# Inverse transform of two batches on 193 columns for a token and its mirror, in a kernel of attention and a gated long convolution

## Chip, cores and metric

The kernel runs on one core of a Trainium2 chip. The metric is the device time of one execution in microseconds (us), lower is better. The core has TensorE (PE: matmuls, with PEld for the weight loads that run beside them), VectorE (DVE), ScalarE (ACT), GpSimd (POOL) and SyncE (SP, here the issuer of most DMAs). Each engine takes its own instructions strictly in program order and waits on semaphores for the others.

## What is computed

Four batches, eight heads, 768 tokens, head size 64. Heads 0, 2 and 6 attend causally to everything, the others to a window of 64 tokens and 4 sink tokens. The attention output `x` of shape (4, 768, 512) goes through a gated convolution over the tokens:

```python
a = softmax(mask(q @ k.T / sqrt(64)))
x = (a @ v).transpose(0, 2, 1, 3).reshape(B, S, 512)
x1, x2, x3 = split(x @ w_proj, 3)                  # 512 channels each
X2 = rfft(x2, axis=1); H = rfft(filter_fft, axis=0)
y = x1 * irfft(X2 * H, n=S, axis=1) * x3
out = y @ w_out
```

## The kernel before

The tokens are split into two halves of 384 (`HS`), the transform is done as matmuls with tables of cosines and sines. Work is cut into small named operations; a long list, `FAST`, names every one of them in the order in which it is issued, so each engine's queue is that list without the other engines' entries. A suffix picks the engine where there is a choice (`/v` VectorE, `/s` ScalarE, `/p` GpSimd) and `@0` to `@3` picks one of four PSUM slots of two banks. A slot is free again when its last reader is done.

For each pair of heads `n` (0 to 15, four to a batch):
- `lq`, `lk`, `lv` load q, k, v (SP); `cq`, `ck` or `cqk`, and `cv{n}`, convert them to bf16. Up to n = 7 PE turns q and k (`T{n}.a`, emptied by `E`); from n = 8 a DMA does (`T{n}`, L962, on SP).
- `sc` are the score matmuls (L990), `sb` adds masks by matmul for the first pairs, `ex` is the exponential on ScalarE, `mk`/`mr` are masks on VectorE, `vx`, `vs`, `ks` prepare window and sink entries.
- `at` is probabilities times values, `rec` and `nm` divide by the sums (L1067, VectorE) and give `attn`.
- `fd`, `fe` fold the two halves of the tokens (difference and sum); from n = 5 `fA`, `fS`, `fb`, `fr` go further. `W` (L1103 to L1111) transforms attn over the tokens, `We` empties it.
- `tn` transposes attn into `xT`: on PE up to n = 10, by a DMA on SP (L1132) from n = 11.

For each batch `b`:
- `X{b}.t.u` multiplies the transformed attention with the x2 columns of w_proj (L1154), `Xe` empties it, `sw` swaps two halves of one piece by DMA; `pa`, `pb`, `pc` multiply with the filter's spectrum `HAB` and leave `P`.
- for each block `cb` of 128 channels: `x1`, `x3` are the two other projections (L1189; `xs` empties x1, `g` multiplies with x3). `c{b}.{cb}.r` is the inverse transform (L1227), for r = 0 and 1: three matmuls with 384 columns of the table `Gi` each. Their sum and difference are the two halves of the tokens: `ce` copies the r = 0 part to SBUF, and two operations `cv{b}.{cb}.half` (L1238) add and subtract the r = 1 part straight from PSUM. `y` multiplies in the remaining factor.
- `o{b}.{i}` are the output matmuls (L1262), `oe` empties them, `st` stores them. The last token block of batch 3 is done in two halves of the columns (L1257).

In the opening, `lfilt` loads the filter and `lw{part}.{hh}` the six pieces of w_proj; these DMAs are issued by GpSimd and stand in its queue (L776, L784). Piece `lw1.*` is what `X` needs, `lw0.*` and `lw2.*` are for `x1` and `x3`. `fold1` and `fold0` (L797, L793) fold the filter on VectorE, `F` transforms it, `H` scales it into `HAB`. Eight matmuls with no use, `rest` (L586), follow the last output matmul. `gd0` to `gd4` check the softmax sums: three VectorE operations, one matmul (`gd3`, L669) and a VectorE operation that writes a word `other` (`gd4`, L674). Every engine reads that word at the end (L1314) and branches on it.

Of the kernel before, what the change touches and what calls it, by code (L numbers as in the profile page):

```python
# [68 lines left out]
cv1/s nm0/v ex2.0 lw1.1 Ge0/v Gt1@3 sc1.2@1 ex2.1 ks2/s vs1/v Gh0 sb1.2 vx1/s sc2.4@0 ex1.2 T3.0@2 T3.1 lq4 Ge1/v lk4
fd0/v E3.0/v lw1.0 ex2.4 lq6 sc2.3@3 at1.1@1 fe0/v sc2.2@0 at1.0 E3.1/v rec1 sb2.2 nm1/v ex2.3 W0.1@3 cv2/s cv3/p  # L70
vx3/s ex2.2 fe1/v tn0@2 W0.0 te0/s sc3.1@1 sb3.1 vx2/v fd1/v at2.0@0 ck5/p vs2/s sc3.0@2 at2.1 We0/v lv4 cq5/s ks3/s
T5.1@3 cq4/p sb3.0 T5.0 ex3.1 sc3.2@1 sb3.2 rec2 nm2/v fe2/p E5.0/v ck4/p E5.1/v ex3.0 Gh1 W1.0@0 lv5 ex3.2 T4.0@2
E4.0/s W1.1 tn2@1 lq7 vs3/v tn1@3 We1/s T4.1 te2/v sc5.0@1 sc5.1@0 lk6 te1/v at3.1@3 fold1 at3.0 E4.1/s fold0 rec3
ex5.0 F2.1@2 ex5.1 sc4.4@1 nm3/v F2.0 ex4.4 sc4.5@0 ex4.5 fd2/v fd3/p sc4.2@3 ex4.2 F0.1@1 W2.1@0 W2.0 H2.0/v fe3/p
H0.2/s We2/s H2.2/v F1.1@3 F0.0 W3.1@0 H1.2/s lw0.0 H0.1/s H2.1/v ks5/p W3.0 cq6/v mk4.2 We3/v F1.0 H0.0/s H1.1/s
sc5.2@2 sc4.3@1 ex4.3 cv4/v X0.2.1@0 lw0.1 X0.2.0 H1.0/v sc4.1@1 sc4.0@3 lw2.0 mk5.0 ex5.2 X0.1.0@2 Xe0.2/s cv5/v
X0.1.1 ex4.0 X0.0.1@0 ex4.1 mk4.1 ck6/v vx5/v tn3@3 lk7 mk4.0 vs5/v X0.0.0 Xe0.1/s te3/s mk5.2 T6.0@1 Xe0.0/s Hd1
cq7/p lw2.1 T7.0@2 T6.1 mk5.1 ck7/v T7.1 at5.1@3 H2.5 pb0.1/v E7.0/v Hd0 at5.0 E6.1/s sw0.0 rec5 at4.1@0 E6.0/s at4.0
# [15 lines left out]
ks11/v pa1.1/p sc10.2@2 vx10/s sc11.2@0 X1.0.0 g1.0 sw1.0 vs10/v vs11/v ex10.2 x11.2.0@1 pb1.1/v fe9/v lq14 Xe1.0/s
mr10 fb8/v mk10.0 fS9/v mk10.2 x11.2.1 o0.4.0@2 mk11.1 ex11.2 tn9@3 xs1.2/s at10.0@0 at10.1 mk11.0 lq13 mk11.2 fA9/v
x11.1.0@1 x11.1.1 o0.5.0 o0.4.1 o0.5.1 fb9/p vx11/s rec10 cqk12/s nm10/v at11.0@0 at11.1 fr9 te9/s fr8 fd10/p
x31.1.0@3 T12 oe0.5/s W9.1@2 W9.0 xs1.1/s pb1.2/v x31.1.1 rec11 nm11/v tn10@1 pc1.1/v We9/s W8.1@0 tn11 W8.0 te10/s
g1.1 pa1.0/v sc12.1@2 pa1.2/v sc12.4@3 x31.2.1@1 x31.2.0 We8/s sc12.0@0 fe10/v pc1.2/v fe11/p ex12.1 x12.0.0@2 g1.2
fS10/p fA10/p lk13 ex12.4 x12.0.1 ex12.0 x32.0.0@3 pb1.0/v lv12 fb10/p pc1.0/v xs2.0/s sc12.5@1 sc12.2@0 fd11/v
sc12.3@2 x32.0.1 ex12.5 c1.0.0@1 c1.0.1 ex12.2 fr10 fA11/v lq15 fS11/v W10.1@0 W10.0 ex12.3 fr11 c1.1.0@2 c1.1.1  # L100
fb11/p g2.0 ce1.0/s c1.2.0@3 We10/s ce1.1/s W11.0@0 cv1.0.1 cv13/p cv1.0.0 mk12.1 cv1.1.0 cv1.1.1 c1.3.1@1 cqk13/s
W11.1 c1.3.0 y1.1/v y1.0/v ce1.3/v lk14 We11/s c1.2.1 ce1.2/s cv1.3.0 X2.1.0@2 lk15 T13 cv1.3.1 cqk14/s cv1.2.1
cv12/s X2.0.0@0 X2.1.1 mk12.0 X2.0.1 x31.3.0@1 T14 mk12.2 Xe2.1/s x31.3.1 Xe2.0/s cv1.2.0 y1.3/v sc13.1@3 vs13/s
# [5 lines left out]
fA13/v x12.2.0 cv14/v sw2.0 vs14/s cv15/v x12.1.0@3 o1.2.0@0 tn13 xs2.2/s mk15.0 vx15/s st1.1 mk14.0 o1.3.0 fb13/v
vs15/v fb12/v x12.1.1 oe1.5/s W12.1@1 mr14 mk15.1 fr13 mk14.2 W12.0 o1.3.1 o1.2.1 vx14/s at14.0@2 xs2.1/s mk15.2  # L110
W13.1@3 W13.0 st1.5 We12/s at14.1 oe1.3/s at15.0@1 pc2.1/v pb2.2/v We13/s at15.1 rec14 rec15 pc2.2/p x32.1.0@0
x32.1.1 nm14/v c2.1.0@3 nm15/v c2.1.1 tn14 st1.3 ce2.1/s g2.1 cv2.1.1 cv2.1.0 c2.0.0@2 ce2.0/s c2.2.1@1 fd14/p y2.1/v
c2.3.1@0 fe15/p c2.3.0 c2.2.0 ce2.3/s fd15/v x32.2.1@3 cv2.3.1 cv2.3.0 fe14/p c2.0.1 x32.2.0 cv2.0.1 tn15 fS15/p
fS14/p fA14/p x32.3.1@0 cv2.0.0 x13.1.1@2 fA15/p ce2.2/s x13.1.0 g2.2 x32.3.0 xs3.1/s fr14 fb15/v y2.0/v fb14/v
W14.0@3 W14.1 x13.0.1@2 We14/s cv2.2.0 fr15 x13.0.0 W15.0@3 W15.1 cv2.2.1 x33.0.1@1 We15/v x33.0.0 y2.2/p X3.2.1@3
X3.2.0 xs3.0/s Xe3.2/s X3.1.1@2 y2.3/v g3.0 X3.1.0 X3.0.1@1 sw3.1 g2.3 Xe3.1/s sw3.0 X3.0.0 x13.2.1@0 pa3.1/v Xe3.0/s
o2.1.0@3 x13.3.0@2 o2.0.0 pa3.2/p x33.2.0@1 x13.2.0 pb3.1/p x13.3.1 pb3.2/v gd0 pc3.2/v o2.1.1 xs3.2/s pa3.0/v
pb3.0/v x33.2.1 x33.1.0@0 pc3.1/v o2.0.1 xs3.3/s g3.2 c3.0.0@2 pc3.0/p x33.1.1 c3.1.0@1 oe2.1/s ce3.0/s o2.4.0@3 g3.1
gd1 c3.0.1 c3.2.1@0 c3.1.1 c3.2.0 o2.5.0 cv3.0.1 cv3.0.0 c3.3.0@2 ce3.1/s gd2 cv3.1.1 cv3.1.0 y3.0/p o2.5.1 o2.4.1
ce3.2/s y3.1/p c3.3.1 cv3.2.0 st2.1 oe2.5/s o2.3.0@1 o2.2.0 cv3.2.1 o2.3.1 o2.2.1 ce3.3/s cv3.3.1 x33.3.1@0 oe2.3/s  # L120
cv3.3.0 x33.3.0 y3.2/v st2.5 st2.3 gd3@3 o3.0.0@2 o3.4.0@1 y3.3/v g3.3 gh o3.0.1 gd4 oe3.0/s o3.4.1 o3.1.0@0 o3.1.1
o3.2.0@3 o3.2.1 o3.3.0@2 oe3.1/s o3.3.1 oe3.4/v st3.0/v oe3.2/s oe3.3/s o3.5.1@1 st3.4/v st3.1/v oe3.6/s o3.5.0@0
oe3.5/s st3.6/s st3.2/v st3.3/v st3.5/v rest@3 late
"""
# [1274 lines left out]
```

## Time and profile before

| | |
|---|---|
| times of three runs | 185.31, 184.15, 185.63 us; median 185.31 |
| span of the profiled execution, first to last instruction | 182.1 us |
| the profiled execution's own time outside the span | not given by the page; the median is 3.2 us above the span |
| busy: PE, DVE, ACT, POOL | 172.8, 149.8, 145.3, 77.5 us |
| TensorE clock granted | 1.000 |

The views used are: the share of each engine; the chain of work that ended last (start, length, what); groups of instructions (line, engine, operation, output<-inputs, shape, count, then busy us, mean ns of one, then idle time ahead and who ended it); the timeline (start, length, engine, line, operation, then in brackets the wait ahead of it); stretches of the span with the busy time of each engine; DMA issues with their time to landing; and single lines with first and last start.

### The profile page before, as it was taken

Reading aid. Unit: us, or ns where it says so; the run is one execution under the profiler, and the core shown is the slowest. Engines: PE = TensorE matmul, PEld = TensorE weight load, DVE = VectorE, ACT = ScalarE, POOL = GpSimd, SP = SyncE. Lnnn points to the kernel's source line nnn. Section 1 sums busy time; section 2 is a strip of 40 time slices with the busy share of each in tenths; the row PEclk is TensorE's granted clock in tenths of the full one; section 3 lists DMA queues with packets and bytes.
Section 4 is the critical chain, followed back from the end, with each engine's and each line's share of the span. In section 5 each row is a group of like instructions: output and inputs, shape, how many; then the busy total and the mean of one; then the engine's idle time right before and its main releaser. Section 6 shows DMA issues by size and latency. Waiting matters only on the chain.

```text
span 182.1 us, 4374 instructions
## 1 busy us (share of the span) xinstructions
PE 172.8 (95%) x1684; PEld 103.6 (57%) x1700; DVE 149.8 (82%) x298; ACT 145.3 (80%) x196; POOL 77.5 (43%) x94
## 2 busy tenths in 40 slices
...
GB/s 159 356 203 287 294 257 200 204 290 230 232 224 166 184 228 198 116 214 142 265 217 200 150 231 166 123 208 243 228 153 112 184 0 0 58 2 119 127 277 184
DMA packets 78396, 33.83 MB, mean 186 GB/s; under 512 B 67618, under 2 KB 74786, under 8 KB 78370
## 3 DMA queue, kind: packets, MB, share of 16 engines
...
q10 hardware_dynamic: 146, 0.13, 0.2%
...
## 4 chain that ended last, share of the span: by engine, by line
PE 82%; DVE 8%; ACT 4%; DMA 3%; issue 1%
PE f_x_ps L1189 23%; PE f_X_ps L1154 12%; PE f_out_ps L1262 10%; PE f_c_ps L1227 9%; PE f_sc L990 8%; PE f_att L1050 7%; DMA f_qkT<-f_qk_bf 3%; PE f_qkT_ps L952 2%; PE f_sc L1001 2%; PE warm L454 2%; PE f_xt_ps L1123 2%; ACT f_pT L1007 1%; DVE f_HAB L691 1%; PE f_W_ps L1103 1%; PE f_W_ps L1105 1%
## 5 line engine op out<-in xcount | busy, mean ns | idle before, releaser
L1007 ACT ACTIVATE f_pT<-f_sc 128x1024 bf16<-128x1024 f32 (+3 forms) x68 | 58.5, 914 | 3.6 <-PE f_sc L990 2.0
L1189 PE MATMUL f_x_ps<-f_xT,f_wproj 128*128 128x384 bf16 x256 | 46.9, 326 | 0.0
L1189 PEld LDWEIGHTS <-f_wproj 128*128 128x128 bf16 x256 | 23.9, 98 | 17.4 <-issue 1.6
L990 PE MATMUL f_sc<-f_qkT 64*128 64x128 bf16 (+3 forms) x328 | 20.9, 242 | 2.4 <-DMA f_qkT<-f_qk_bf 1.4
L1154 PE MATMUL f_X_ps<-f_wproj,f_xh 128*128 128x512 bf16 x90 | 22.1, 379 | 0.6 <-issue 0.2
L544 POOL TENSOR_TENSOR f_fo<-f_attn 128x384 bf16<-128x384 bf16 x15 | 14.6, 990 | 18.4 <-DVE f_attn L1067 17.3
L1262 PE MATMUL f_out_ps<-f_wout,f_gy 128*128 128x512 bf16 x86 | 22.0, 379 | 0.3
L990 PEld LDWEIGHTS <-f_qkT 64*128 64x128 bf16 x328 | 11.4, 94 | 13.0 <-issue 7.9
L1238 DVE TENSOR_TENSOR turns<-angle,f_c_ps 128x384 bf16<-128x384 f32 x32 | 16.3, 550 | 2.6 <-ACT angle L541 1.3
L1227 PE MATMUL f_c_ps<-f_Gi,f_P 128*128 128x384 bf16 x96 | 18.2, 326 | 0.1
L1050 PEld LDWEIGHTS <-f_pT 128*128 128x128 bf16 x472 | 16.2, 97 | 2.4 <-issue 0.4
L1050 PE MATMUL f_att<-f_v_aug,f_pT 128*128 128x65 bf16 x392 | 17.0, 193 | 0.0
L541 ACT COPY f_o<-f_out_ps 128x1024 f32<-128x1024 f32 (+2 forms) x15 | 12.1, 818 | 6.2 <-PE f_out_ps L1262 5.1
L541 ACT CAST f_X<-f_X_ps 128x1024 bf16<-128x1024 f32 x12 | 12.1, 1016 | 4.9 <-PE f_X_ps L1154 4.9
L1067 DVE TENSOR_TENSOR f_attn<-f_att,f_recs 128x768 bf16<-128x768 f32 x16 | 15.1, 951 | 0.6
L544 POOL TENSOR_TENSOR f_P<-f_X,f_HAB 128x1024 bf16<-128x1024 bf16 x4 | 8.9, 2215 | 14.5 <-ACT f_X L541 14.5
L544 POOL TENSOR_TENSOR f_gy<-turns,f_gy 128x768 bf16<-128x768 bf16 x5 | 8.5, 1710 | 14.6 <-DVE turns L1238 14.6
L1154 PEld LDWEIGHTS <-f_xh 128*128 128x128 bf16 x96 | 8.9, 97 | 10.2 <-issue 0.5
L1262 PEld LDWEIGHTS <-f_gy 128*128 128x128 bf16 x92 | 8.5, 98 | 8.8 <-POOL f_uv L544 0.4
L541 ACT COPY angle<-f_c_ps 128x384 f32<-128x384 f32 x15 | 7.2, 478 | 7.7 <-PE f_c_ps L1227 5.4
L1227 PEld LDWEIGHTS <-f_P 128*128 128x128 bf16 x96 | 9.1, 98 | 6.0 <-issue 0.2
L537 POOL CAST f_qk_bf<-qk_ahead 128x768 bf16<-128x768 f32 (+1 forms) x9 | 8.0, 900 | 8.7 <-DMA qk_ahead<-in_k_dram 3.4
...
## 6 DMA issues: line engine op xcount, KB each, us to landing
...
out_dram<-f_o SPq DMA_DIRECT2D x17, 256.0 KB, 2.4
...
f_wproj<-in_moe_w_proj_dram POOLq DMA_DIRECT2D x6, 256.0 KB, 8.2
out_dram<-f_o SPq DMA_DIRECT2D x3, 512.0 KB, 4.4
```

Of the source, the lines that this page charges most:

```text
L537: nc.gpsimd.tensor_copy(out=out, in_=in_)
L541: nc.scalar.copy(out=out, in_=in_)
L544: (nc.gpsimd if now["engine"] == "p" else nc.vector).tensor_tensor(out, a, b, op)
L990: nc.tensor.matmul(sc[:, bank, col:col + 128 * cnt], lhsT=keys, rhs=qkT(n)[rows, 0, 128 * i:128 * (i + cnt)], start=(col == 0 or not biase ...
L1007: nc.scalar.activation(out=pT(n)[:, c, :, 0:w], in_=held[f"sc.{n}.{c}"][:, :, 0:w], func=AF.Exp, scale=SCALE)
L1050: nc.tensor.matmul(att[:, hh, 65 * i:65 * i + 65], lhsT=pT(n)[:, c, bank, col:col + 128], rhs=values, start=(z == 0), stop=(z == len(here) ...
L1067: nc.vector.tensor_mul(attn(n).rearrange("p i hh d -> p hh i d"), rows[:, :, :, 0:64], recs()[:, n][:, :, :, None].to_broadcast([128, 2, N ...
L1154: nc.tensor.matmul(ps[:, u, :], lhsT=xh(b)[:, cc, chain, 128 * part:128 * part + 128], rhs=wproj()[:, cc, DM:2 * DM], start=(cc == 0), sto ...
L1189: nc.tensor.matmul(ps[:, s, 0:HS], lhsT=wproj()[:, cc, part * DM + cb * 128:part * DM + (cb + 1) * 128], rhs=xT(b)[:, cc, s * HS:s * HS + HS],
L1227: nc.tensor.matmul(ps[:, r, 0:HS], lhsT=P(b)[:, t, u, ch], rhs=Gi()[:, tile_no], start=(m == 0), stop=(m == 2))
L1238: fn(conv[:, half * HS:half * HS + HS], held[f"evs.{b}.{cb}"], held[f"c_ps.{b}.{cb}"][:, 1, 0:HS])
L1262: nc.tensor.matmul(ps[:, i % 2, :], lhsT=gy(b)[:, cb, i * 128:(i + 1) * 128], rhs=wout()[:, cb, :], start=(cb == 0), stop=(cb == NC - 1))
```

## The change

For batches 2 and 3 the inverse transform is done on 193 columns. Its tables have symmetries: the value at token n and at its mirror, 768 - n, are the same up to sign, once cosine and sine terms are kept apart. So the first two of the three tables are used on columns 0 to 192 alone and give two partial results side by side in one bank, of 193 columns each. The third table holds cosines and sines in one tile (rows 0 to 63 and 64 to 127); a new table `Gb` (128 x 2 x 2 x 194, bf16) has its rows laid apart with zeros elsewhere, so that one matmul of 386 columns adds to both. `Gb` is made by a memset (`Gz`), two copies (`Gb0`, `Gb1`) and a correction of one row (`Gn`).

`ce` now copies 386 columns, the two `cv` write sum and difference of 386 columns each in fp32 to SBUF, and two new VectorE operations per block, `cw{b}.{cb}.half`, add and subtract the 193-column parts from each other, the second one reading backwards, and write `conv`. That is 16 operations more. They use the buffers of the first two loads of q and k.

The filter's real part is no longer stored twice in `HAB` for t = 0 and 1; `pa` reads it through a broadcast.

The core of the diff:

```diff
+    Gb = C("Gb", [128, 2, 2, 194], BF16)
...
+    wave = lambda part, rows, tiles: Gi()[rows, tiles].rearrange("p t m f -> p t (m f)")[:, :, 0:193]
+    @op("Gz")
+        (nc.gpsimd if now["engine"] == "p" else nc.vector).memset(Gb(), 0.0)
+    for half in range(2):
+        @op(f"Gb{half}")
+            rows = slice(64 * half, 64 * half + 64)
+            ev(Gb()[rows, :, half, 0:193], wave(half, rows, slice(2, 6, 3)))
+    @op("Gn")
+        nc.vector.tensor_copy(out=Gb()[64:65, 1, 0, 0:193], in_=wave(0, slice(64, 65), slice(5, 6))[:, 0])
+        nc.vector.memset(Gb()[64:65, 1, 1], 0.0)
...
-        scaled(f"H{t}.0", lambda t=t: HAB()[:, t, 0:2, :],
-               lambda t=t: FP(t)[:, 0, None, :].to_broadcast([128, 2, DM]), 2.0 / S)
+        scaled(f"H{t}.0", lambda t=t: HAB()[:, t, 0, :], lambda t=t: FP(t)[:, 0], 2.0 / S)
...
-                two(P(b)[:, t], held[f"X.{b}.{t}"], HAB()[:, t, 0:2], ALU.mult)
+                real = HAB()[:, t, 0:2] if t == 2 else HAB()[:, t, 0, None].to_broadcast([128, 2, DM])
+                two(P(b)[:, t], held[f"X.{b}.{t}"], real, ALU.mult)
...
+                    if b in MIRROR:                                   # MIRROR = (2, 3)
+                        both = ps[:, r, 0:386].rearrange("p (h n) -> p h n", h=2)
+                        nc.tensor.matmul(both, lhsT=P(b)[:, t2, u2, ch], rhs=Gb()[:, shared_tile // 3, :, 0:193],
+                                         start=True, stop=False, skip_group_check=True)
+                        nc.tensor.matmul(both[:, 0], lhsT=P(b)[:, t0, u0, ch], rhs=waves(a), start=False, stop=True, ...)
+                        nc.tensor.matmul(both[:, 1], lhsT=P(b)[:, t1, u1, ch], rhs=waves(z), start=False, stop=True, ...)
+                        return
...
+                        fn(parts[:, half, 0:386], even[:, 0:386], held[f"c_ps.{b}.{cb}"][:, 1, 0:386])       # cv
...
+                        if half == 0:                                                                       # cw
+                            two(conv[:, :, 0:192], parts[:, :, 0:192], parts[:, :, 193:385], ALU.add)
+                        else:
+                            two(conv[:, :, 192:384], parts[:, ::-1, 192:0:-1], parts[:, ::-1, 385:193:-1], ALU.subtract)
```

With this the whole list `FAST` is a new one: all operations stand in another order, and 130 of those that can run on several engines have another engine. The places that the prediction speaks of, old and new (three dots stand for other operations):

```diff
-... ck3/p ... cq3/p ... at0.0@3 at0.1 ... lfilt ... lw1.1 ... lw1.0 ... at3.1@3 fold1 at3.0 ... fold0 rec3 ... F2.1@2 ... nm3/v ... fe3/p ... X0.2.1@0
+... at0.0@3 at0.1 ... nm0/v ... ck3/p fd0/p ... cv2/p ... ks2/p ... Gz/p ... lfilt ... lw1.0 ... fold1 ... fold0 rec3 F2.1@3 ... nm3/v ... fd2/p ... fe3/p ... lw1.1 ... X0.2.1@0
-... cqk12/s nm10/v at11.0@0 ... T12 ... nm11/v ... tn11 ... sc12.1@2 sc12.4@3 ... sc12.0@0 ... x12.0.0@2
+... cqk12/p ... T12 ... nm11/v ... sc12.1@2 ... sc12.4@3 ... sc12.0@1 ... tn11 ... x12.0.0@2
+... fr13 We12/s c2.1.0@0 g2.1 c2.1.1 ce2.1/s cv2.1.1 cv2.1.0 cw2.1.1/v cw2.1.0/v c2.3.0@2 ... y2.1/v ... fr14 W14.0@3 cw2.3.1/v ... fr15 W14.1 cw2.0.1/v We14/s fb15/v W15.0@0 cw2.0.0/v W15.1 y2.0/p ...
+... pc3.0/v c3.1.1 ce3.1/s ... g3.1 cv3.1.0 cv3.1.1 cw3.1.1/v ... cw3.0.1/v ce3.3/s ce3.2/s y3.1/p y3.0/p cv3.3.0 ... cw3.2.1/v y3.2/v o3.4.0@3 y3.3/v g3.3 o3.0.0@2 o3.4.1 gh gd0 gd1 ...
-... gd2 ... gd3@3 o3.0.0@2 ... gh o3.0.1 gd4 ... o3.5.1@1 ... oe3.6/s o3.5.0@0 oe3.5/s st3.6/s st3.2/v st3.3/v st3.5/v rest@3 late
+... o3.3.1 st3.1/v oe3.3/s oe3.2/v o3.5.1@1 st3.2/v rest@2 st3.3/v gd2 gd3@2 oe3.6/v st3.6/s late gd4
```

More of the change, by code (lines that the diff above doesn't have):

```diff
@@ L69 @@
[L69 to L78, printed above, removed]
@@ L94 @@
[L94 to L103, printed above, removed]
@@ L109 @@
[L109 to L123, printed above, removed]
+ones1 kz2/v lq2 wrap0 sin2 ones0 blank3@2 alt size cos2 mtab3 ck0/s cq2/p T0.1@3 cq0/v cos1 gs0/v lk2 btab sin1 gs2/p
@@ new lines @@
+vx1/v lk5 lv3 fe0/v te0/v sb2.2 T3.1@0 lk4 E3.1/s T3.0 E3.0/v W0.1@3 Gh1 ex2.2 ck5/s W0.0 lfilt vs2/v lw1.0 at1.1@2
+vx2/p We0/v at1.0 rec1 sc3.1@0 sc3.0@1 sb3.0 ks3/p ex3.0 sb3.1 at2.1@3 at2.0 nm1/v cv3/p sc3.2@1 cq5/p ex3.1 sb3.2
+T5.0@2 T5.1 vx3/s ex3.2 fe1/v E5.1/s fd1/p W1.0@0 rec2 nm2/v E5.0/v ck4/p lq4 lk7 W1.1 We1/s tn2@1 te2/v cq4/p T4.1@3
+tn1@2 te1/v T4.0 E4.1/s lq6 sc5.0@0 lv5 fold1 sc5.1@1 vs3/p at3.0@2 E4.0/s ex5.0 at3.1 ex5.1 fold0 rec3 F2.1@3 ks5/p
+sc4.4@0 F2.0 sc4.5@1 nm3/v lq7 fe2/v fd2/p H2.1/v H2.2/v fe3/p sc4.2@2 ex4.4 F0.1@0 lw1.1 ex4.5 W2.0@1 H2.0/s F0.0
@@ new lines @@
+mk11.1 pa1.0/v x11.1.1@1 mk10.1 tn9@0 ex11.2 o0.5.1 vx10/p te9/s pa1.2/v fb9/v mk10.2 o0.4.1 x11.1.0 sw1.0 W9.0@0
+mk11.2 at10.1@3 oe0.5/s mr10 mk11.0 vs11/v xs1.1/s lk13 at10.0 rec10 x11.2.0@2 x11.2.1 xs1.2/s nm10/v W9.1 at11.1@1
+pb1.2/p at11.0 x31.1.0@3 x31.1.1 We9/s lv14 rec11 fd10/p nm11/v g1.1 cv14/s tn10@0 fe10/p W8.1@1 W8.0 pa1.1/v sc12.1@2
+lq15 te10/s fe11/v sc12.4@3 fd11/p We8/s fS10/v x31.2.0@0 fA10/v lk15 fb10/p sc12.0@1 x31.2.1 tn11 ex12.1 fS11/p
+ex12.0 pc1.2/v x12.0.0@2 lk14 lq14 x12.0.1 lv13 ex12.4 g1.2 xs2.0/s vx14/s x32.0.0@1 fr10 sc12.5@3 pb1.0/v pc1.1/v
```

106 lines of the change are left out of this document (78 added, 28 removed).

## Prediction

> **What bounds the kernel now.** I read the share of each engine first, then the chain that ended last, then stretches of the span, because a share over the whole span hides which engine ends a stage.
>
> ```profile
> PE 172.8 (95%) x1684; PEld 103.6 (57%) x1700; DVE 149.8 (82%) x298; ACT 145.3 (80%) x196; POOL 77.5 (43%) x94
> PE 82%; DVE 8%; ACT 4%; DMA 3%; issue 1%
> 139.80:151.50 11.70, 11.69 (x78) 7.27 (x76) 9.96 (x20) 4.31 (x7) 6.65 (x8) 1.00 0.42 80
> 151.50:164.10 12.60, 12.49 (x67) 6.55 (x68) 8.81 (x11) 5.65 (x7) 7.12 (x3) 1.00 0.09 21
> 164.10:172.30 8.20, 8.20 (x47) 4.30 (x46) 6.50 (x13) 3.64 (x6) 3.27 (x3) 1.00 0.35 130
> ```
>
> TensorE (PE) carries 82% of the chain. The three stretches run from the first inverse transform of batch 2 to the first output matmul of batch 3; after the length come busy us of PE, weight loads, VectorE (DVE), ScalarE (ACT), GpSimd (POOL), then the clock. PE is never free there, at full clock, and DVE is busy 25.3 of 32.5 us. So a matmul taken away pays here only as far as DVE's 7.2 free us carry what DVE is given.
>
> The opening is different. Where the chain crosses 30 to 40 us it runs through DVE, with two weight DMAs close behind:
>
> ```profile
> 30.88 1.02 DVE f_xT L535 x2
> 31.90 0.86 DVE f_fold L797
> 32.76 0.87 DVE f_fold L793
> 33.63 0.15 DVE f_recs L1056
> 33.81 0.96 DVE f_attn L1067
> ...
> 40.51 0.81 PE f_X_ps L1154 x3
> ```
>
> PE starts the spectrum of batch 0 (X0.2.1) at 40.51 only when this DVE row is through.
>
> The profiled execution has a span of 182.1 us; the median of the timed runs is 185.31. I take the 3.2 us between them as unchanged and sum against the span. Under 1% (1.85 us) a measurement of this kernel can't be told from no change.
>
> **Term 1, the matmuls: -2.6 us.** Each of the 16 inverse operations of batches 2 and 3 changes from three matmuls of 384 columns to one of 386 and two of 193.
>
> ```profile
> 96.48 1.30 PE f_x_ps L1189 x8
> 30.50 0.35 PE f_xt_ps L1123 x6
> 119.68 1.39 PE f_att L1050 x42
> ```
>
> The spacing is 162 ns for 384 columns (1.30/8), 58 ns for 128 (0.35/6) and 33 ns for 65, each of the last with its own weight load, so weights don't set a floor at 193. A straight line gives 163 ns for 386 and 82 ns for 193: 327 instead of 487 ns, 160 saved, 16 times 2.56 us. If 193 columns cost what 256 would by that line (109 ns), 1.7 us is left.
>
> **Term 2, VectorE in the last two batches: +1.8 us.** The sums and differences cv now write 386 fp32 columns, two more than before, which I cost at nothing. New are 16 operations cw on 2x192 fp32 elements, both inputs in SBUF, half of them reading backwards. The trace has none; the nearest rows:
>
> ```profile
> L1238 DVE TENSOR_TENSOR turns<-angle,f_c_ps 128x384 bf16<-128x384 f32 x32 | 16.3, 550 | 2.6 <-ACT angle L541 1.3 <-PE f_c_ps L1227 0.5 <-POOL f_gy L544 0.3
> L544 DVE TENSOR_TENSOR f_fo<-f_attn 128x384 bf16<-128x384 bf16 x17 | 6.8, 407 | 0.1
> L679 DVE SCALAR_TENSOR_TENSOR angle<-turns,angle 128x384 f32<-128x384 int32 x1 | 0.6, 557 | 0.7 <-ACT turns L462 0.7
> ```
>
> 384 elements take 407 ns in bf16 and 557 ns with two 32-bit inputs in SBUF. The cv average 510 ns a piece in busy time (16.3/32), overlap taken off; I take 0.50, nearest the 32-bit row, and keep 0.40 and 0.56 as ends. That is 8.0 us (6.4 to 9.0). The sequence also hands DVE pa3.2, pb3.1 and pc3.0, and takes y2.0, y2.3, fd15, fb14, We15 and the three guard steps gd0 to gd2 out of this stretch:
>
> ```profile
> L544 DVE TENSOR_TENSOR f_m<-f_X,f_HAB 128x1024 bf16<-128x1024 bf16 x7 | 4.7, 674 | 0.0
> L544 DVE TENSOR_TENSOR turns<-turns,f_x1s 128x768 bf16<-128x768 bf16 x4 | 2.3, 567 | 0.0
> L535 DVE CAST f_xh<-f_W_ps 128x768 bf16<-128x768 f32 x4 | 3.8, 956 | 1.6 <-PE f_W_ps L1107 1.5
> ```
>
> In: 3 x 0.67 = 2.0. Out: two y at 0.57, the fold fd15 at 0.40 (6.8/17), the smaller sum fb14 at 0.3, We15 at 0.96 and three guards on 192 elements, by the 407 ns row no more than 0.3 each: 3.7. DVE's demand becomes 25.3 + 8.0 + 2.0 - 3.7 = 31.6 us, while PE's stretch would shrink to 32.5 - 2.6 = 29.9. DVE becomes the bound: at least 1.7 of the 2.6 us comes back as PE waiting, and I write 1.8. With the cheap cw it is 0.1; DVE's own waits come on top (first rival). Behind a late cw stand conv, y, then the output matmuls; the weights of W14 and W15 wait behind it too, since fr14, fr15 and fb15 stand among the cw in DVE's queue.
>
> Small pieces cost nothing where I see cover: Gb0 and Gb1 are two ACT copies of half the rows, Gn two DVE operations, and the broadcast in pa replaces stored copies at equal width. H0.0 and H1.0 write half as much. If the cover fails, they are under 1 us together.
>
> **Term 3, the opening: +1.5 us.** The filter load lfilt moves behind fd0, cv2, ks2 and the new memset Gz in POOL's queue, and the weight load lw1.1 behind fe3, which waits for nm3.
>
> ```profile
> 17.33 1.59 POOL L537 CAST f_qk_bf<-qk_ahead 128x768 bf16<-128x768 f32 x2 [3.20 <-DMA qk_ahead<-in_k_dram]
> 18.86 1.04 POOL L776 DMA_DIRECT2D f_filt<-in_moe_filter_fft_dram  x1
> ...
> 34.91 1.78 POOL L544 TENSOR_TENSOR f_fo<-f_attn 128x384 bf16<-128x384 bf16 x2 [4.60 <-DVE f_attn L1067]
> 36.64 0.62 POOL L784 DMA_DIRECT2D f_wproj<-in_moe_w_proj_dram  x1
> f_filt<-in_moe_filter_fft_dram POOLq DMA_DIRECT2D x1, 768.0 KB, 12.7
> f_wproj<-in_moe_w_proj_dram POOLq DMA_DIRECT2D x1, 256.0 KB, 7.3
> f_wout<-in_moe_w_out_dram POOLq DMA_DIRECT2D x1, 512.0 KB, 5.5
> ```
>
> The filter landed at 18.86 + 12.7 = 31.6, and fold1 began at 31.8: no slack. POOL is held by a key load until 17.33 as before. One cast then takes 0.8; fd0 is a fold like those at 34.91 (0.9 each), and cv2, ks2 and Gz, a cast, a small copy and a memset, take together between one and three times that, so lfilt is issued between 20 and 22; I take 21. By 12.7 us it lands near 34; less stands behind it in its queue than the two weight loads of before, so I take 33, 1.2 us late. nm3 follows fold1 by 2.9 us (rows above), fe3 takes 0.9, so lw1.1 is issued near 37 and lands between 42.3 (5.5 us, the landing on a calm queue) and 44.1 (7.3). X0 needs both halves. Some 0.9 us of matmuls now stand ahead of X0.2.1 that stood behind it, so X0 would be due at 41.4; it is 0.9 to 2.7 late, and I take 1.5. The lower end is -1: with less on DVE and ACT ahead of the fold, the opening may gain if both loads come early.
>
> The Trainium skill ("DMA: Bandwidth & Descriptors", section "Anatomy of one DMA — SWDGE (gpsimd) path") fits such a load as 2.0 us plus its bytes at 436 GB/s. By that fit, an estimate, 256 KB land in 2.6 us, nothing is late and the sum is 1.5 lower. The row of 7.3 us speaks against it on this busy queue.
>
> **Term 4, the stall of PE at 103 us: -0.5 us.**
>
> ```profile
> 103.66 0.61 PE L990 MATMUL f_sc<-f_qkT 64*128 64x256 bf16 x6 [1.40 <-DMA f_qkT<-f_qk_bf]
> 100.82 1.21 SPq L1132 DMA_TRANSPOSE f_xT<-f_attn  x1
> f_xT<-f_attn SPq DMA_TRANSPOSE x1, 3.7
> ```
>
> cqk12 and T12 move some 7 us of PE work ahead, so the 1.40 us wait for the transposed keys goes. Next late is tn11: nm11 stays 3.5 us of PE work ahead of x12.0.0, and its transpose, issued at 100.82, lands at 104.5. x12.0.0 follows the six score matmuls above, at 104.3; without the 1.40 it comes at 102.9, uses tn11's part in its fourth matmul (at 103.4), and waits 0.9 to 1.1 there. Of 1.4 about 0.5 is left. Ends: -1.4 and 0.
>
> **Term 5, the end: +1.3 us.** gd3 and gd4 move behind the eight closing matmuls `rest`, and every engine reads gd4's word before the program may end.
>
> ```profile
> 177.65 1.73 PE f_rest_ps L586 x8
> 173.27 0.20 DVE L674 TENSOR_SCALAR other<-f_rows_right,differ 1x1 int32<-1x1 f32 x1
> 178.08 0.33 SPq L1280 DMA_DIRECT2D out_dram<-f_o  x1
> out_dram<-f_o SPq DMA_DIRECT2D x1, 128.0 KB, 2.9
> L1314 SPq TENSOR_LOAD <-other x1: 772/772/772, 178.5 to 178.5; - x1
> L1394 SPq EVENT_SEMAPHORE  x14: 17/28/28, 180.2 to 182.1; - x14
> ```
>
> Today the word is ready at 173.5, and the last store (178.08 + 2.9 = 181.0) ends the span 1.1 us later. Count from the end of the output matmuls, E = 177.65; the span ends at E + 4.45. After the change: rest to E + 1.73, gd3 0.2, gd4 0.2 and hand-overs 0.15 make E + 2.3; SP's read to its first semaphore takes 1.7, its semaphores 1.7 without the wait for the store: E + 5.7. Bounds 0.6 and 1.6.
>
> **Sum.** -2.6 + 1.8 + 1.5 - 0.5 + 1.3 = +1.5: a span of 183.6, a time of **186.8 us**, inside the 1%. My forecast is no change that can be told, on its slow side.
>
> **Rivals.**
> - **The port that DVE and POOL share (slower), 189.3 us.** Some operations with both inputs in SBUF wait until POOL's is over:
>
> ```profile
> 156.43 2.57 POOL L544 TENSOR_TENSOR f_m<-f_X,f_HAB 128x1024 bf16<-128x1024 bf16 x1
> 157.20 2.35 DVE L544 TENSOR_TENSOR f_m<-f_Xw,f_HAB 128x1024 bf16<-128x1024 bf16 x1 [0.18 <-DMA f_Xw<-f_X]
> ```
>
>   An operation of 0.67 us took 2.35 and ended 0.55 after POOL's (159.00). The old cv read PSUM; all 16 cw are of the blocked kind, and POOL runs eight folds and sums and three y beside the cw of batch 2, and two y beside those of batch 3. At half a fold (0.5 us) each blocked cw lengthens the stage that DVE bounds; one takes the sum past 1%, and I take five, 2.5 us. Against it: many DVE operations beside POOL took their usual time. The Trainium skill ("SBUF — State Buffer", section "Who interferes with whom") states it as an exclusive lock between a DVE instruction with two SBUF inputs and a GpSimd one that reads SBUF; by that rule the trace agrees at 157.20.
> - **Both late loads at their worst (slower), 188.8 us.** lfilt at 34 and lw1.1 at 45: 3.5 instead of 1.5.
> - **Cover holds (faster), 183.3 us.** Loads land in time, cw fit into DVE's gaps at 0.40: -2.6 + 0.1 - 0.5 + 1.3 - 0.3 = -2.0. The 7.2 free us speak for it.
> - **The matmuls gain less:** 1.7 for 2.6 gives 187.7, if DVE didn't bind; it does, so the time hardly moves.
>
> **Chances.** Forecast 0.42; shared port 0.25; late loads 0.13; cover 0.18; little gain on PE 0.02. So faster by over 1% 0.18, within 1% 0.42, slower 0.40. The range runs from 183.2 (faster case) to 189.4 (port case); about 1 in 10 is left on each side.
>
> **What would show it.** Term 1: 16 matmuls of 386 and 32 of 193, spaced 163 and 82 ns. Term 2: DVE above 95% from 140 us to the first output matmul, waits of PE on DVE there; cw near 550 ns, longer ones only beside POOL. Term 3: fold1 waiting for the filter's DMA near 32, X0 for the weights near 42. Term 4: no wait at sc12, one at x12.0.0. Term 5: gd4 two us behind the last output matmul, SP's semaphores unblocked. I am wrong if X0 starts by 41 us, or if DVE shows gaps in the last 40 us while PE doesn't wait.

## The result, and the profile after

The changed kernel takes 203.04 us (median of four runs, 202.57 to 203.42) against 185.09 before: 1.105 times, 95% interval 1.096 to 1.113. Forecast were 186.8 us and a range up to 189.4. Times of a kernel with several executions are, from here on, medians of those within 1.5% of its fastest one, while the recorded expectations on e6, e8, e9, e11 and e18 still go by medians of all (194.3 and 9.8 us for e2_mirror). The executions of the kernel before whose time and span are both on record take 1.4 to 1.7 us longer than their span, and the profiled one of the changed kernel 1.5 (202.88 and 201.4). So the 3.2 us that the prediction found outside the span are no constant: by these figures the profiled execution of before took about 183.6 us (an estimate), less than the median. That is why the spans differ by 19.3 us and the medians by 18.0.

The page of the changed kernel, span, engine shares and the chain by engine:

```profile
span 201.4 us, 4415 instructions
PE 173.8 (86%) x1684; PEld 103.2 (51%) x1700; DVE 169.9 (84%) x308; ACT 138.3 (69%) x183; POOL 96.1 (48%) x118
DVE 40%; PE 31%; ACT 11%; DMA 6%; issue 6%; POOL 1%; SPq 1%; ACTq 0%; DVEq 0%
```

TensorE's busy time stayed nearly the same, its share of the chain fell from 82% to 31%. VectorE is busy 20.1 us longer, GpSimd 18.6, ScalarE 7.0 less. The 16 cw are only 12.1 of VectorE's 20.1.

Next I cut both kernels at matmuls that both have. Single lines, with first and last start; first the kernel before (spectrum X, inverse c), then the changed one (X; c of batches 0 and 1; the 386 and 193 columns of batches 2 and 3; the halved output block):

```profile
L1154 PE MATMUL f_X_ps<-f_wproj,f_xh x90: 376/379/390, 40.5 to 156.3; 128*128 128x512 bf16 x90
L1227 PE MATMUL f_c_ps<-f_Gi,f_P x96: 322/326/336, 62.0 to 168.9; 128*128 128x384 bf16 x96
L1257 PE MATMUL f_out_ps<-f_wout,f_gy x8: 273/273/273, 176.6 to 177.4; 128*128 128x256 bf16 x8
```

```profile
L1173 PE MATMUL f_X_ps<-f_wproj,f_xh x89: 376/379/389, 44.8 to 169.1; 128*128 128x512 bf16 x89
L1258 PE MATMUL f_c_ps<-f_Gi,f_P x48: 322/326/337, 69.6 to 123.7; 128*128 128x384 bf16 x48
L1250 PE MATMUL f_c_ps<-f_Gb,f_P x16: 324/327/338, 151.0 to 178.9; 128*128 128x386 bf16 x16
L1252 PE MATMUL f_c_ps<-f_Gi,f_P x16: 244/247/258, 151.2 to 179.1; 128*128 128x193 bf16 x16
L1312 PE MATMUL f_out_ps<-f_wout,f_gy x8: 269/272/273, 187.9 to 191.6; 128*128 128x256 bf16 x8
```

These lines don't tell the output matmuls of batch 2 from those of batch 3, so that cut is read from the order of time, before and then changed. In both kernels the last 8 output matmuls of batch 2 (o2.2, o2.3) and the 8 of x33.3 come first, and o3 follows them:

```profile
170.79 1.46 PE L1189 MATMUL f_x_ps<-f_xT,f_wproj 128*128 128x384 bf16 x8
172.28 4.49 PE L1262 MATMUL f_out_ps<-f_wout,f_gy 128*128 128x512 bf16 x19
```

```profile
182.83 1.90 PE L1317 MATMUL f_out_ps<-f_wout,f_gy 128*128 128x512 bf16 x8 [1.28 <-DVE qk_ahead L1273]
184.56 1.46 PE L1209 MATMUL f_x_ps<-f_xT,f_wproj 128*128 128x384 bf16 x8
185.87 0.38 PE L1317 MATMUL f_out_ps<-f_wout,f_gy 128*128 128x512 bf16 x1
```

| us | before | changed | lost in the stretch |
|---|---|---|---|
| first X of batch 0 | 40.5 | 44.8 | 4.3 |
| first c of batch 0 | 62.0 | 69.6 | 3.3 |
| first c of batch 2 | 139.7 | 151.0 | 3.7 |
| first output matmul of batch 3 | 172.3 | 185.9 | 2.3 |
| last output matmul | 177.4 | 191.6 | 0.6 |
| end of the span | 182.1 | 201.4 | 5.1 |

Every stretch got longer, and 11.3 us are lost before the first changed matmul runs. The stretch that the change is about, from the first c of batch 2 to the first output matmul of batch 3, is 2.3 us longer: VectorE is busy there for 33.2 of 34.9 us, and PE waits 3.5 us. (The orders differ, so a stretch does not hold quite the same matmuls: the six of W13, 0.5 us, stand ahead of the first c of batch 2 before and behind it in the changed kernel.) The stretches of the span (columns as in the prediction) for batches 0 and 1, before and after, and then that of the inverse of batches 2 and 3, after:

```profile
62.00:139.70 77.70, 75.50 (x809) 46.95 (x815) 69.74 (x152) 73.01 (x94) 29.41 (x29) 1.00 0.98 190
```

```profile
69.60:151.00 81.40, 75.47 (x794) 45.60 (x798) 77.45 (x137) 65.73 (x86) 43.22 (x42) 1.00 0.81 171
151.00:185.87 34.87, 31.07 (x193) 18.03 (x196) 33.22 (x60) 15.05 (x21) 14.70 (x14) 1.00 0.19 59
```

In batches 0 and 1, with not one cw in them, the new sequence took 7.3 us from ScalarE and gave 13.8 to GpSimd, and VectorE, with 15 operations fewer, is busy 7.7 us longer: 95% of the stretch. How fewer operations can take longer shows at one place in the order of time, VectorE first, then GpSimd:

```profile
91.40 1.88 DVE L1044 TENSOR_TENSOR f_pT<-f_pT,mtab 128x768 bf16<-128x768 bf16 x2
93.21 1.54 DVE L537 COPY f_v_x<-f_v_aug 4x520 bf16<-4x520 bf16 x1
```

```profile
91.13 1.61 POOL L546 TENSOR_TENSOR f_uv<-f_fo 128x256 bf16<-128x256 bf16 x2
92.69 1.92 POOL L539 CAST f_qk_bf<-qk_ahead 128x1536 bf16<-128x1536 f32 x1
```

A copy of four rows lasts 1.54 us and ends 0.1 us behind GpSimd's cast (92.69 + 1.92 = 94.61). PE waits 1.3 us for it. That looks like the prediction's port rival, in a stretch for which it had no price; the run e3 below tests it.

### The profile page after: what moved, and what is told of

Read it like the earlier page. It is cut to its first block, busy times and chain, and to the rows that moved or that the text cites. A ratio compares the mean times of both kernels' runs of the same rounds, so it can differ in the third digit from the quotient of the medians.

```text
span 201.4 us, 4415 instructions
## 1 busy us (share of the span) xinstructions
PE 173.8 (86%) x1684; PEld 103.2 (51%) x1700; DVE 169.9 (84%) x308; ACT 138.3 (69%) x183; POOL 96.1 (48%) x118
## 4 chain that ended last, share of the span: by engine, by line
DVE 40%; PE 31%; ACT 11%; DMA 6%; issue 6%; POOL 1%; SPq 1%; ACTq 0%; DVEq 0%
PE f_x_ps L1209 10%; DVE turns L546 5%; ACT f_pT L1026 4%; PE f_sc L1009 4%; DVE f_P L546 4%; DMA qk_ahead<-in_q_dram 4%; DVE f_pT L1044 3%; PE f_att L1069 3%; DVE qk_ahead L1273 3%; DVE f_m L546 3%; PE f_out_ps L1317 3%; DVE f_attn L1086 2%; DMA f_qkT<-f_qk_bf 2%; DVE f_gy L1228 2%; DVE f_qkT L537 2%
## 5 line engine op out<-in xcount | busy, mean ns | idle before, releaser
L546 POOL TENSOR_TENSOR f_fo<-f_attn 128x384 bf16<-128x384 bf16 x17 | 17.8, 1057 | 13.4 <-DVE f_attn L1086 11.8
L546 POOL TENSOR_TENSOR f_gy<-turns,f_gy 128x768 bf16<-128x768 bf16 x7 | 11.6, 1662 | 15.1 <-DVE turns L546 15.0
L546 POOL TENSOR_TENSOR f_uv<-f_fo 128x256 bf16<-128x256 bf16 x12 | 8.4, 712 | 20.9 <-DVE f_fo L546 19.0
L543 ACT CAST f_X<-f_X_ps 128x1024 bf16<-128x1024 f32 x10 | 10.1, 1012 | 8.5 <-PE f_X_ps L1173 8.5
L543 ACT COPY f_o<-f_out_ps 128x1024 f32<-128x1024 f32 (+1 forms) x11 | 9.9, 897 | 8.0 <-PE f_out_ps L1317 6.3
L1044 DVE TENSOR_TENSOR f_pT<-f_pT,mtab 128x1024 bf16<-128x1024 bf16 (+1 forms) x18 | 12.7, 716 | 0.0
L537 DVE COPY f_qkT<-f_qkT_ps 128x768 bf16<-128x768 bf16 x8 | 7.5, 952 | 5.9 <-PE f_qkT_ps L971 4.3
L546 POOL TENSOR_TENSOR f_br<-f_fo,f_uv 128x256 bf16<-128x256 bf16 x7 | 7.9, 1128 | 9.5 <-DVE f_uv L546 5.9
L546 DVE TENSOR_TENSOR turns<-qk_ahead 128x384 bf16<-128x384 f32 x16 | 12.1, 784 | 0.2
L543 ACT CAST f_xh<-f_W_ps 128x768 bf16<-128x768 f32 x12 | 9.6, 804 | 1.5 <-PE f_W_ps L1126 1.5
```

What stands on the lines that cost most here:

```text
L537: nc.vector.tensor_copy(out=out, in_=in_)
L543: nc.scalar.copy(out=out, in_=in_)
L546: (nc.gpsimd if now["engine"] == "p" else nc.vector).tensor_tensor(out, a, b, op)
L1044: nc.vector.tensor_mul(some, some, tab.to_broadcast([128, 2, cols, 128]))
```

## The experiments

**Order or mirror.** Two runs part them: the new sequence with the old inverse, and the old sequence with the new inverse.

```diff
# e1_order: the changed kernel
-MIRROR = (2, 3)
+MIRROR = ()
- Gz/p Gb0/s Gb1/s Gn and the 16 cw in FAST
# e2_mirror: the changed kernel, with the FAST of before and in it
+ ... lw2.1 Gz/p ... xs1.0/s Gb1/s ... xs1.2/s Gb0/s ... cv12/s Gn ... cv2.1.1 cv2.1.0 cw2.1.1/v cw2.1.0/v ...
```

> The changed kernel's sequence with the old inverse in all batches: three matmuls of 384 columns, no cw, no table Gb. VectorE loses the 16 cw (12.1 us busy) and Gn (1.4), TensorE gets 2.6 us back. Theory 'sequence' (the new order and its engine choices cost most of the 18 us, cw or not): 196 to 203. Theory 'mirror' (the sums and differences overload VectorE, the order is innocent): 185 to 190.

> The old sequence with the new inverse: each cw pair stands directly behind its cv pair on VectorE, the memset Gz is with GpSimd in the opening behind the last weight load, the two copies Gb and Gn follow during batch 1 and 2. All other places and engines are those of before. Theory 'sequence': terms 1 and 2 of the prediction alone, 183.5 to 186. Theory 'mirror': VectorE binds the last 40 us and the time is 193 or more.

e1_order took 204.01 us (1.1105 times before, 1.102 to 1.119), 1 us more than theory 'sequence' had. One sum buffer is overwritten there before it is used (cv of block 3 precedes y of block 1 in batch 2); that changes values, no work. So the sequence by itself costs all of it, and the mirror's theory falls for the changed kernel. Its stretch from the first c of batch 2 to the first output matmul of batch 3:

```profile
151.14:187.54 36.40, 33.33 (x192) 18.49 (x195) 25.75 (x46) 15.20 (x21) 14.92 (x14) 1.00 0.18 57
```

With the old inverse the new sequence needs 36.4 us there, 3.8 more than before; with the mirror it needs 34.9. In this sequence the mirror thus gives 1.5 us back in the profile; in the whole time the 1.0 us between the two runs is inside their intervals.

e2_mirror took 192.5 (192.40 and 192.66) against 184.3: 8.2 us, just below the 193 of theory 'mirror' and far above 'sequence'. The two prices do not add up. In e1_order the waits show up on other operations, here fr14 and fr15 (0.42 us each in the kernel before, mean of 11), while GpSimd runs y:

```profile
159.81 2.67 DVE L1112 SCALAR_TENSOR_TENSOR f_br<-f_uv,f_fo 128x256 bf16<-128x256 bf16 x2
```

```profile
160.37 1.82 POOL L544 TENSOR_TENSOR f_gy<-turns,f_gy 128x768 bf16<-128x768 bf16 x1
162.15 1.82 POOL L544 TENSOR_TENSOR turns<-turns,f_x1s 128x768 bf16<-128x768 bf16 x1
```

Without the cw, the next two-input operation is the one that lasts longer.

**Port or load.** GpSimd stays as long busy but hardly reads:

```diff
# e3_pool_blind_after (the changed kernel), e4_pool_blind_before (the kernel before)
     def two(out, a, b, op):
-        (nc.gpsimd if now["engine"] == "p" else nc.vector).tensor_tensor(out, a, b, op)
+        if now["engine"] == "p":                  # thin: the first element of each row
+            nc.gpsimd.tensor_tensor(thin(out), thin(a), thin(b), op)
+            nc.gpsimd.memset(out, 0.0)            # and a second memset of 3/4 of it
+            ...
# the same for GpSimd's copies and casts of 256 elements and more
```

> The changed kernel, but GpSimd's sums, products and casts of 256 elements and more read only one element of each row and then fill their output by memsets of about the same duration: GpSimd is as long busy, but reads nearly nothing. The values of these tiles are left out (zeros). Theory 'port' (VectorE is blocked by GpSimd's reading: in the changed kernel its operations last 18.9 us longer than the same shapes usually do, 8.7 before): most of that goes, cw fall from 784 to about 550 ns, and the time falls to 191 to 197. Theory 'load' (VectorE simply has more to do): cw stay above 700 ns and the time at 200 to 204.

> The control: the kernel before with the same replacement of GpSimd's reading by memsets (values left out). Its TensorE has only 7.6 us of gaps, so both theories expect 182 to 185.5; theory 'port' that VectorE's busy time falls by some 6 us with little effect on the time, theory 'load' that it stays at 150.

The changed kernel falls to 194.9 (1.060 times before, 1.052 to 1.069), 8.1 us less; the kernel before does not gain (185.92, 1.005 to 1.025 times), though its VectorE is busy 144.9 instead of 149.8 us. The cw by shape, changed kernel and e3, then the stretch of batches 0 and 1 and that of the mirror in e3:

```profile
L546 DVE TENSOR_TENSOR turns<-qk_ahead 128x384 bf16<-128x384 f32 x16 | 12.1, 784 | 0.2
```

```profile
L565 DVE TENSOR_TENSOR turns<-qk_ahead 128x384 bf16<-128x384 f32 x16 | 8.3, 552 | 0.2
```

```profile
69.90:145.60 75.70, 73.88 (x792) 45.32 (x797) 66.44 (x136) 65.23 (x86) 42.01 (x106) 1.00 0.95 189
145.63:178.51 32.88, 30.79 (x194) 17.86 (x195) 29.02 (x61) 15.00 (x21) 14.96 (x41) 1.00 0.19 57
```

With GpSimd nearly as busy as in the changed kernel (42.0 against 43.2 us), VectorE is done with the same work in 66.4 us instead of 77.5, and the stretch is 5.7 us shorter, 2.0 shorter than before the change. Another 2.0 are gained in the stretch of the mirror (32.9 instead of 34.9). Theory 'port' holds. The Trainium skill ("SBUF — State Buffer", section "Who interferes with whom") says that a VectorE instruction with two SBUF inputs contends with a GpSimd one that reads SBUF and not with one that only writes, and that copies can contend too; by it the trace agrees (784 to 552 ns; the four-row copy of 1.54 us above falls to 0.28 in e3).

**The guard.**

```diff
# e5_guard_early
- ... gh gd0 gd1 oe3.4/s o3.5.0@1 ... st3.3/v gd2 gd3@2 oe3.6/v st3.6/s late gd4
+ ... gh gd0 gd1 gd2 oe3.4/s gd3@0 o3.5.0@1 oe3.5/v gd4 o3.0.1 ... st3.3/v oe3.6/v st3.6/s late
# e14_guard_mid
+ ... gh gd0 gd1 oe3.4/s o3.5.0@1 oe3.5/v gd2 o3.0.1 oe3.0/s o3.1.0@0 o3.1.1 gd3@3 ... oe3.1/v gd4 ... late
```

> The changed kernel with gd2, gd3 and gd4 moved ahead of the output matmuls o3.5.0 and o3.0.1, as gd3 and gd4 stood before; all else as in the changed kernel. There the span ends 9.6 us after the last output matmul, before 4.5. Theory 'guard' (the word read last makes the end late, above all GpSimd's, whose drain stands 3.9 us behind its last branch): about 4 us come back, 198 to 200. Theory 'end' (something else in the last 10 us, stores or the eight closing matmuls, is as late): 202 or more.

> The changed kernel with gd2 behind oe3.5, gd3 behind o3.1.1 and gd4 behind oe3.1, each where VectorE waits for output matmuls anyway. Theory 'guard': the output matmuls end as in the changed kernel (191.8) and the span 4.5 us later, as before: span 196 to 197, time 197.5 to 199. Theory 'end': the span still ends 7 us or more behind the last output matmul, 201 or more.

e5 took 200.12 (1.081 to 1.100 times before), e14 197.65 (1.069 to 1.082): 2.9 and 5.4 us less, e5 at the edge of what theory 'guard' had and e14 inside it. In e5 the end is as short as before (last output matmul 194.5, span 198.7), but gd3 stands ahead of output matmuls and waits 1.0 us for gd2, with others behind it, and these matmuls end 2.9 later. e14 has no such wait. Which engine is late shows at the last line of each kernel; the word and GpSimd's way from it, before, changed and e14:

```profile
L674 DVE TENSOR_SCALAR other<-f_rows_right,differ x1: 199/199/199, 173.3 to 173.3; 1x1 int32<-1x1 f32 x1
L1394 POOLq DRAIN  x3: 40/107/803, 175.7 to 181.8; - x3
```

```profile
L677 DVE TENSOR_SCALAR other<-f_rows_right,differ x1: 205/205/205, 194.1 to 194.1; 1x1 int32<-1x1 f32 x1
L1449 SPq DRAIN  x3: 7/7/13, 196.6 to 200.8; - x3
L1449 POOLq DRAIN  x3: 40/107/807, 199.7 to 201.1; - x3
```

```profile
L677 DVE TENSOR_SCALAR other<-f_rows_right,differ x1: 196/196/196, 190.4 to 190.4; 1x1 int32<-1x1 f32 x1
L1449 SPq DRAIN  x3: 7/7/13, 195.7 to 196.3; - x3
L1449 POOLq DRAIN  x3: 40/107/807, 195.2 to 196.6; - x3
```

In the changed kernel SP comes to its first drain 2.5 us after the word (196.6), and GpSimd to its first 3.1 us after that (199.7); the other engines are there by 195.7. SP's queue waits 4.1 us there, until GpSimd's drain is over; the view puts that wait down to PE's queue, which had long drained, so that it is GpSimd is read from the order of time. GpSimd needs 2.4, 5.6 and 4.8 us from word to drain; an early word hides them behind output matmuls. What it does in that time the profile does not show.

**Engines or order.**

```diff
# e6_old_engines: the FAST of after, each of the 130 changed suffixes as before
- cqk12/p ... y3.1/p ...      + cqk12/s ... (as before)
# e7_new_engines: the kernel before, its 130 suffixes as after
```

> The changed kernel's order and new inverse, but the 130 operations with another engine are back on their engine of before. Theory 'engines' (work moved from ScalarE to GpSimd and VectorE, 13 us more on GpSimd, is what the sequence costs): 191 to 196, near the run of the new inverse in the old sequence (194.3). Theory 'order' (the order itself makes the engines wait, in the opening above all): 199 to 206.

> The kernel before, its order and its inverse, but the 130 operations on the engines that the changed kernel gives them. Theory 'engines': 195 to 203. Theory 'order': 184 to 189.

They took 232.0 (1.252 to 1.274) and 211.6 (1.142 to 1.170). Both theories missed: each cross is worse than either kernel. A foreign half makes new waits, so these runs decide nothing between order and engines.

**The opening.**

```diff
# e10_old_opening: the 230 operations of before up to X0.2.1, then what is left of the changed order
# e13_old_opening2: cut at X0.1.0, and at the seam
- ... lk7 ck7/s ... X0.1.0@2 ...
+ ... lk6 lk7 ... X0.1.0@2 ... lq8 ck7/s ck6/v ...
```

> The changed kernel with the opening of before: all operations up to the first spectrum matmul X0.2.1 in the old order and on the old engines (230 operations), then what is left in the changed kernel's order. There X0.2.1 starts at 44.8, before at 40.5. Theory 'opening' (the order and the engines ahead of X0 cost these 4 us, and nothing later takes them back): X0.2.1 near 41, time 198 to 200. Theory 'later bound' (VectorE bounds what follows, an earlier X0 waits there): 202 or more.

> The changed kernel with the opening of before up to X0.1.0 (239 operations in the old order and on the old engines), then the changed kernel's order; at the seam the load lk7 stands early and the cast ck7 behind X0.1, so that no filter operation waits for it. Theory 'opening': X0.2.1 at 41 instead of 44.8, and nothing later takes the gain back: 198 to 200. Theory 'later bound' (VectorE and GpSimd bound what follows): 202 or more although X0.2.1 is early.

e10 (206.69, 1.110 to 1.130) failed at its seam: a cast waits on ScalarE 2.5 us for its load, a filter operation stands behind it, and PE waits 5.7 us. From 40 to 60 us TensorE was then granted 0.83 of its clock. As X started later than in the changed kernel (47.0), this run tests neither theory. e13 mends the seam and gains nothing: 203.36 (1.099 to 1.113), though X starts early:

```profile
L1173 PE MATMUL f_X_ps<-f_wproj,f_xh x89: 376/379/389, 42.1 to 168.8; 128*128 128x512 bf16 x89
L1258 PE MATMUL f_c_ps<-f_Gi,f_P x48: 323/326/336, 69.2 to 123.4; 128*128 128x384 bf16 x48
```

2.7 us earlier at X are 0.4 at the first c: theory 'later bound'. The order from X on binds (in both the longest wait of PE from 40 to 70 us is for VectorE's copy of the turned keys, 1.5 and 1.6 us), so the 4.3 us at X were no price of their own.

**All three at once.**

> The changed kernel with three things undone at once: the old opening up to X0.2.1, the guard steps early, and GpSimd's large operations reading nearly nothing (values left out, as in the run of that alone). If the three causes add up: 203 - 2.9 - 8.1 - 4 = 188 (186.5 to 190). If they overlap (two of them pay for the same wait): 191 to 195.

> The changed kernel with all three undone: the opening of before with the mended seam, the guard in the middle of the output matmuls, and GpSimd's large operations reading nearly nothing (values left out). If opening (4), guard (4.5) and port (8.1) add up: 203 - 16.6 = 186.4, 185 to 188.5, about the old sequence. If they overlap: 190 to 194.

e12 has e10's seam and e5's guard and says little (194.3). e16, with e13's opening, e14's guard and the blind GpSimd, took 190.42 (1.029 to 1.043). That is inside what was expected for causes that overlap. Port 8.1 and guard 5.4 are 13.5, measured are 12.6: these two nearly add up, and of the opening's 4 us nothing is left. Against the control e4 (185.92) 4.5 us stay; in the profile they lie between X and the first c (40.4 to 66.6; before 40.5 to 62.0).

**The mirror in the old sequence.**

```diff
# e8_mirror2, e9_mirror3: e2_mirror with
+MIRROR = (2,)    # and (3,)
# e11_half_parts: e2_mirror with
-                parts = space[:, 0:772].rearrange("p (z n) -> p z n", z=2)
+                parts = space[:, 0:386].bitcast(BF16).rearrange("p (z n) -> p z n", z=2)
# e18_mirror_blind: e2_mirror with the two() of e3
```

> The old sequence with the new inverse in batch 2 alone (8 cw instead of 16), batch 3 as before. With both batches TensorE's gaps were 4.5 us longer from 140 to 155 and 5 us longer from 170 to 185. Theory 'burst' (in each batch the chain of matmul, cv, cw and y is on the path by itself, whatever VectorE's mean share): about half of the 9.8 us, 188 to 190.5. Theory 'mean load' (VectorE's free time in the last 40 us takes up 4 us of cw): 183.5 to 186.

> The old sequence with the new inverse in batch 3 alone; batch 2 as before. Batch 2 alone cost 4.2 us, both 9.8. Theory 'burst': the rest, 4.5 to 6 us, so 188.5 to 190.5. Theory 'mean load' (eight cw fit into VectorE's free time, the second eight no longer): 184 to 186.5.

> The old sequence with the new inverse in both batches (194.3), but cv writes its sums and differences in bf16 instead of fp32, so that cw reads two bf16 inputs (its result is rounded once more). Theory 'burst': cw fall from 660 to some 400 ns and the time follows by half or more of 16 x 0.2 = 3 us: 191 to 193. Theory 'port alone' (a cw's length is GpSimd's): 193.5 to 195.

> The old sequence with the new inverse in both batches (194.3), GpSimd's large operations reading nearly nothing as in the two earlier runs of that (values left out; the kernel before takes 185.9 so). Theory 'port' (GpSimd's reading makes the mirror's chain late): 186 to 189. Theory 'chain' (the sums and differences hang one behind the other on VectorE, 550 ns each, GpSimd or not): 190.5 to 193.5.

Batch 2 alone costs 1.019 times (1.007 to 1.031), 3.5 us; batch 3 alone 2.8 us (187.25, from one execution only). Both lie between the ranges of the two theories. By 'mean load' less should have been lost (186.0 and 186.5 at most), so each batch pays for itself, as theory 'burst' says, but less than it had. In the profiles both together cost 8.7 us of span. Of these, 2.2 lie ahead of the first c of batch 2 (141.9; before 139.7): fold1 waited 1.5 us for the filter's load, and X started at 43.1. The order up to X is that of before, and e8, e9 and e11, which share it, start X at 40.5 to 41.0, so this is no price of the mirror. From the first c of batch 2 to the end e2 takes 48.9 us and the kernel before 42.4: 6.5 us. The waits of PE behind 139.8 us in e2, and the stretch of its first inverse transforms:

```profile
PE f_x_ps L1209 <- DVE qk_ahead L1273: 3.4, 3, 2.0
PE f_out_ps L1317 <- DVE f_gy L546: 1.1, 1, 1.1
PE f_out_ps L1317 <- DVE qk_ahead L1273: 1.1, 1, 1.1
```

```profile
141.90:155.00 13.10, 9.31 (x64) 5.47 (x63) 12.93 (x26) 3.43 (x6) 5.77 (x7) 1.00 0.36 71
```

Where four blocks come together, VectorE is full (12.93 of 13.10) and PE waits until a cv frees the PSUM slot of the next matmul. The mean of VectorE over the last 40 us hides that. With bf16 parts (e11: 188.0, 1.021 to 1.036 times, below what either theory had) cw fall from 660 to 462 ns; from the first c of batch 2 to the end the profile gives 46.3 instead of 48.9 us. These 2.6 us are what I ascribe to the edit; the rest of the gain lies ahead of that c, which the edit doesn't touch. e18 takes 191.2 (1.030 to 1.047 times), as 'chain' had it. From the first c of batch 2 to the end it is 4.3 us longer than its control e4 (46.9 and 42.6), so of the 6.5 us there the chain is the larger part and the port the rest.

**Term 4 by itself.**

```diff
# e15_T12 (FAST of before)
+ ... x11.2.1 cqk12/s ... x11.1.1 T12 ...
# e17_load12
+ ... lv11 lk12 lq12 ... xs1.2/s cqk12/s T12 ...
```

> The kernel before with one step moved: the cast cqk12 behind the matmul x11.2.1 and the transposing DMA T12 behind x11.1.1, some 5 us earlier; all else as before. By term 4 of the prediction the 1.40 us wait for the transposed keys goes and about 1 us of it returns at x12.0.0 as a wait for tn11: span 0.3 to 0.6 shorter, 184.0. Theory 'all': nothing is late behind it, 1.4 us: 183. Theory 'nothing' (the DMA is late through its queue, not its place): the wait stays, 184.4.

> The kernel before with the loads lk12 and lq12 moved ahead in SP's queue (behind the load lv11), the cast cqk12 and the transposing DMA T12 directly behind xs1.2; all else as before. ScalarE then finds the queries landed. By term 4: the 1.40 us wait for the transposed keys goes and part of it returns at x12.0.0: span 0.3 to 0.6 shorter, ratio about 0.997. Theory 'all' (nothing is late behind it): span 1.2 to 1.5 shorter, ratio 0.992 to 0.994. Theory 'elsewhere' (the other loads, now later in the queue, or the exponentials pay for it): no gain or slower.

Neither gains: 185.7 (1.005 to 1.018) and 186.85 (1.006 to 1.020), some 1% above the kernel before. In e17 that is theory 'elsewhere'; e15 met none of its three. The wait moved; e15, then e17, waits of PE:

```profile
PE f_att L1049 <- ACT f_pT L1006: 2.2, 1, 2.2
```

```profile
PE f_sc L989 <- DMA f_qkT<-f_qk_bf: 1.3, 1, 1.3
```

In e15 the cast waits on ScalarE for its load and the exponentials behind it are late; in e17 the loads stand ahead of the previous pair's transposing DMA, and PE waits at 90 us for that.

None of the versions beats the kernel before.

## Why the prediction was wrong

- **The step that failed is the sum's frame.** It priced the new order at a few named places and left the rest at nothing without a reason, though 130 operations had another engine. Of the 19.3 us of span, 3.7 are lost in batches 0 and 1, 3.3 between X and the first c and 0.6 among the last output matmuls, in stretches for which the sum had no loss. The sequence alone (e1) costs as much as the whole change. Where the sum had terms, it was too low by 2.8 us at X, 3.1 in the stretch of terms 1 and 2, and 3.8 at the end.
- **Port (rival, 0.25):** the mechanism was right, place and size were wrong. It was priced for five cw, 2.5 us; e3 measured 8.1, of which 5.7 lie where no cw runs and 2.0 beside the cw. The row of before that showed it (2.35 instead of 0.67 us) named no cw either; the work newly given to GpSimd should have been counted stretch by stretch.
- **Term 1, -2.6:** right as the price of the matmuls. 386 columns last 327 ns like 384 (326), 193 columns 247, which by the same overlap of 164 ns is a spacing of 163 and 83 ns. (The 82 ns of the prediction are in proportion to the columns; a line through its rows for 384 and 128 columns gives 85.)
- **Term 2, +1.8:** VectorE did become the bound, 33.2 of 34.9 us, but terms 1 and 2 together, forecast as -0.8, came out as +2.3 against before. The mis-sized part is cw: 784 ns instead of 500, 4.1 us more in all, beyond my upper end of 0.56, which holds without GpSimd's reads (552). The order had no term there, and e1 shows that it takes 3.8 us by itself; against e1 the mirror gains 1.5. In the old sequence the same two terms were +6.5, since I averaged VectorE's free time over 32 us. The broadcast in pa costs nothing, as forecast (682 ns in e3, 671 without it in e4).
- **Term 3, +1.5 by late loads:** wrong mechanism. The filter landed 9.6 us after its issue at 21.6, at 31.2, and fold1 waited until 32.8 for other work of VectorE; lw1.1 landed in 3.9 us at 40.7, with X at 44.8. (The fit of the Trainium skill, "DMA: Bandwidth & Descriptors", section "Anatomy of one DMA — SWDGE (gpsimd) path", gave 2.6 us as an estimate; the measured 3.9 lies between it and the row of 7.3.) By the chain, X was late behind scaling operations that wait for each other on VectorE and ScalarE; no run tested this by itself. The chain of the changed kernel, three dots for what lies between:

```profile
36.32 1.23 DVE f_HAB L694
37.55 1.15 DVE f_Hn L694
38.72 1.50 ACT f_HAB L696 x2
40.22 0.78 ACT f_pT L1026
41.02 0.60 ACT f_HAB L696
...
42.79 0.70 DVE f_HAB L694
```

- **Term 4, -0.5:** the 1.40 us wait is gone in the changed kernel, and so is the one forecast at x12.0.0; in these batches PE waits for VectorE instead. In e3, where PE sets the pace again, x12 waits 1.2 us for tn11 (forecast 0.9 to 1.1):

```profile
PE f_x_ps L1228 <- DMA f_xT<-f_attn: 1.2, 1, 1.2
```

- **Term 5, +1.3:** direction right, size 5.1. The word came 2.5 us behind the start of the last output matmul (forecast 2.3 behind its end) and SP was through about as forecast; I followed SP alone, and GpSimd's first drain came 3.1 us later.

Open stays what binds between X and the first c of batch 0 (4.5 us in e16), and what GpSimd does between the word and its drain.
